# Gated mix of an S4 convolution and a sigmoid GLU: the inverse stage of two pieces in one visit, the first unit fed part by part, results stored in halves, and a new order of work

## The chip, the cores and the metric

The kernel runs on one core of a Trainium2 chip. The metric is the device time of one execution in microseconds (us); less is better. The engines of the core are TensorE (PE, with PEld for its weight loads), VectorE (DVE), ScalarE (ACT), GpSimd (POOL) and SyncE (SP). In this kernel SP issues nearly all transfers (DMAs), and POOL issues the accumulating ones. L12 is line 12 of the kernel; the changed kernel has other line numbers, and where a row of it is shown, the line of before is named beside it.

## The reference

All is in float32. The sequence has 2048 rows of 512 channels, the GLU has 1792 hidden columns, and the state of the convolution has 128 modes for each channel.

```python
g = sigmoid((x * gate_w).sum(-1, keepdims=True))
# a: S4 convolution
dt = exp(log_dt)[:, None];  logdA = dt * A;  dB = dt * Bc
K  = einsum("dn,dnl,dn->dl", Cc, exp(logdA[:, :, None] * l), dB).real      # l = 0 .. 2047
y  = irfft(rfft(u padded) * rfft(K padded))[:, :2048] + u * Dskip
# b: GLU
h = sigmoid(x @ w_gate) * (x @ w_up);   b = h @ w_down
out = g * a + (1 - g) * b
```

The sum over the modes for the table K, the transform, the product with K's transform and the transform back are a; the three large products are b.

## The kernel before

**The GLU.** The 2048 rows are worked in two halves of two blocks (sb 0 and 1) of 512 rows, the hidden columns in 14 groups f of 128. A unit is one (half, sb, f): gate and up (tile `gups`, L947), a sigmoid and a product (L964 on ACT, L966 on DVE), and h (L970, L971). Each float32 operand of the large products is held as a high and a low part, and three matmuls (high by high, high by low, low by high) make one product; so a unit has 2 x 4 x 3 = 24 matmuls of 128x512 on `gups`, and 56 units have 1344. The down product (`dps`, L999) has 672 more of that shape. A loaded 128x512 block lies in a staging tile `st` (DMA L864); ACT writes the high part (L868), DVE the low part (L869).

**The sums.** Down's result for a group of f is scaled by 1 - g and added to a row tile `acc` (L1015 and L1022 on ACT with an accumulating DMA of POOL, L1024; for the last group of the second half L1035 on DVE). Rows of the first half are kept in a buffer in memory and fetched again as `al`.

**The convolution.** The table of K is made by DVE and ACT (`steps`, `pp`, `T`, `B`, `ex`), PE (`kps` L527, `wps` L555) and stored to `a_k`; u's first transform (`ups` L606) is stored to `a_u`. Then come two passes, one for each 256 channels, of 8 pieces p each. A piece loads the constants `wwu` (SP, L653) and `wwv` (L671) and its data `au` (two DMAs, L658) and `ak` (two DMAs, L667); PE makes `s2u` (L688), which is copied to `uf` (L297); PE makes `s2k` (L713), and DVE multiplies the two (L724, L725, L730, L731); PE makes the inverse `ips` (L751) into four banks of PSUM, which are copied to `ev` (L297) and stored to `b_s` (L766). At the end of a pass come the finals: `b_in` is loaded (L789), PE makes `fps` (L801) of it, and DVE adds g times that to the rows: to `al` (load L809, sum L810, store `out<-al` L814) for the first half, and to `acc` (L817) for the second half. What comes last on a row tile of the second half stores it whole (`out<-acc`, 128x512, L829).

These small matmuls use a part of the array each (64x32, 32x64 and so on), while `gups` and `dps` use all of it. A run of `gups` or `dps` is called a full run here, and a run of the others a small run. PSUM's eight banks are three for `gups`, one for `dps` (later it also gets those of `gups`), and four (named XB in the code) for all small tiles.

**The order.** Every part of the work is a generator that yields one step at a time with an engine, a cost, a function and its dependencies. A planner (`Plan.run`) takes the next step of a kind and engine as a table of letters (`ORDER`) says; so the table sets the order of each engine's instructions and of the DMAs in SP's queue. Costs and dependencies only choose which waiting step of a kind is taken and which slot of a buffer it gets. An engine works its queue strictly in this order: if an instruction waits, those behind it wait too, and so do SP's DMAs. The waits themselves go by data and slots.

Of the kernel before, what the change touches and what calls it, by code (L numbers as in the profile page):

```python
# [26 lines left out]
AF = mybir.ActivationFunctionType  # L27
# [24 lines left out]
TURNS = ("ustep PE", "ustep ACT", "ustep -", "inv PE", "inv ACT", "inv SP", "inv -", "x SP", "w SP", "split ACT", "split DVE",  # L52
         "rows PE", "rows ACT", "rows DVE", "rows SP", "rows -", "dn SP", "urest ACT", "urest DVE", "urest SP", "bases ACT",
         "bases DVE", "bases -", "tables PE", "tables DVE", "tables -", "first PE", "first ACT", "first DVE", "first SP", "first -",
         "mags ACT", "mags DVE", "hidden PE", "post ACT", "post DVE", "down PE", "add ACT", "add DVE", "add SP", "add POOL",
         "passes SP", "step PE", "step DVE", "step -", "finals SP", "last PE", "last DVE", "last SP", "last -", "const SP",
         "steps DVE", "steps SP", "preludes ACT", "preludes DVE", "preludes SP", "pw SP", "splitw ACT", "splitw DVE", "splitw SP",
         "splitd ACT", "splitd DVE", "splitd SP")
ORDER = (
    "HJ0zKI56HJzKHJKh4HJhKIQI56hhhhh8zHI56IhhhIHij0JKHQH56ihhJK56h3h3JK569JijKj2hh7ij1y2VVyWPhQh8ijOhhU8VhNijhi9UMPj9UkUyLUVR"  # L60
    "kklhPURhiYOg7YIh5ffikNMIYY6YYjkPLRPONghgklhYhRjgMTg5ikkPLPhVik7VWTIY56hhUYVTjlhUIihkhUkkYYYUYjiYRYONRMPLP3OYN5MPUZIyLTSX"
    "jlkkRhjVTU6iIYgk6PYOhYh55hYbceQNYTYSfj7fgihglRjkaig8kbMkYb!jIhgVlVhiP6YLWUhhhbTPONbVYYkYY9Y5UYYYZi6kMPUTRRUhjILUVPXkj3hh"
    "T!UYi7lOTjY5iYYgYIfjYYfYhRbRNkgTIg7gcYkhQij8hMPe9LPO6kYQ5hgijTRR5hViT6ablhYNbh8hVWbUMPYTbLVhiPkONhhYUYYMTjh!RUYP9kZjXUUT"
    "ViL6UYgRkijjYhhbcQ89kf2Peh!dT6fggOYg1lkkkkgRRiajNlkkYkkib2YYVhbIhhiYMPIVh5YlbkkW5UT6YVbYLUTPONMUPUYRTYL6UYYYYhojRRVoUk7k"
    "IlIRZXbjiYg5fhckjekh7PkYYYkflaoYkYYkohk5YYikYggghbgbhbblVVWU7kI5jhhYiVihUYYYYkYkUUkUoTjIjZXTlk6hiVU6iYh5gffYYjdkIhYYQO8k"
    "Yh6YNMPLYhihhPONRYRjhgiggbgVjVWUk9TMhioYj!yPLhhQ8VYIPcl9eiTRRaYONYk6hh!jQ89!YUQYMih8jTkUbYZXUiPUjjb9iVjb7UYk!YkgLYbYTY5P"
    "lIShYbcfkShkY6hYkefgggkg35oIaYViOoh5lkkVWUk5N6MPT7khIbbVh!7YYhUbiTlkkYYkYYYZLUU6jX6SUVbj5bkl6U!cehYg3RhijkkY2fkhYY12ofTg"
    "YkYlgagkkokkihilkokgdYIboVYYhVbkbWk56UbhVhYYlk!ohUiYUjkToYYjHkYUQUYj8oVkiT9lUZhXQ8jYhgJYYhYQ87bcikYYf9YeaYKHfjog9bbhTkhb"
    "kghibJgl7hHgoJkYVVWkHkYhiUYVlkYojYkKYhYIhYjZUUdpppppUKhUVhpJijiXKQjUCbkYglnYIABBsqppppkYphhceHrYkrHfrfggikrabGYgYhbbjbhY"
    "DEYIYpEhEgVijCHVYWEFJKHABBisqlrhnFprpJhkkUpkVphoprJrihjGUjUDhUnYYYhCKEloEkkJUkYoEYKEFABBYsVUZliqrX!kk3bYgpkYiKp!YrcFfYhe"  # L70
    "rhphjaplfkirYkgYoYpbpjhg3bGbjbDpEEEgYEhCgVVWiiABBQsqrFUVhklrYppprUhFYppQhIhirGYYkUDCEEEYEpFjYhdjjUABYBsqUkrkiiYrnjhpoplV"
    "rFUZhXYbghjY2YhfhckYrYekfYiakYgg12YbgpYlGpgbYhnVbbkVkk!lYDCEpEEYphkkiWUVYAnjEFBBsYFqUiYklpphphjUkpYoZrrprkkrUlXkbckUVGIj"
# [66 lines left out]
class Plan:  # L139
# [62 lines left out]
    def run(self):  # L202
        order, owed = iter(ORDER), []
        turns = dict(zip(LETTERS, TURNS))
        while True:
# [27 lines left out]
            _, n, _, deps = st[2]  # L233
            m = n[eng] if isinstance(n, dict) else n
# [876 lines left out]
```

## Time and profile before

| what | before |
|---|---|
| median of three runs | 625.27 us (624.94 to 626.48) |
| the profiled execution | 625.42 us |
| its span (first to last instruction) | 623.7 us |
| PE busy, share of the span | 608.8 us, 98% |
| DVE busy | 506.4 us, 81% |
| ACT busy | 429.4 us, 69% |
| DMA bytes | 140.34 MB, 225 GB/s on the mean |

The span is the time from the first instruction to the last, and 1.7 us of the profiled execution lie around it. The execution is 0.15 us above the median. A busy time of PE counts modelled ends of pipelined matmuls, so the timeline's starts, not its durations, give the time that a group of matmuls takes. In the timeline a matmul of the small tiles is counted twice as often as in the order lists below (an inverse of 16 matmuls is an `x32`); `gups` and `dps` count alike in both.

### The profile page before, as it was taken

The numbers are of one execution on the slowest core, as the hardware profiler recorded it, in microseconds if no ns is written. First come the engines' busy times: TensorE is split into PE (matmuls) and PEld (weight loads), VectorE is DVE, ScalarE is ACT, GpSimd is POOL, SyncE is SP. The second block draws the span as 40 slices with busy tenths as digits, with TensorE's granted clock in tenths as the row PEclk, the third lists the DMA queues.
The fourth block names the chain that finished last, engine by engine and source line by source line (L and its number), as shares of the span: only waits on it lengthen the run. The fifth ranks groups of instructions, "written<-read, shape, count | busy, mean of one in ns | idle before, by whom it ended". The sixth has DMA issues, their size and how long they took to land.

```text
span 623.7 us, 16354 instructions
## 1 busy us (share of the span) xinstructions
PE 608.8 (98%) x6816; PEld 461.0 (74%) x6816; DVE 506.4 (81%) x902; ACT 429.4 (69%) x726; POOL 35.1 (6%) x44
## 2 busy tenths in 40 slices
PE   5999999999999999999999999999999999998997
PEld 3877777787777778877776777777787776775775
DVE  5879899999999999999999999998986163663145
ACT  5597988989989798988878687767684233342210
POOL 0000000010100111010110000000201000110000
PEclk9999999999999999999999999999999999999999
DMA  7844866588759498698999678777856999999875
GB/s 226 287 161 122 288 204 200 182 234 272 219 158 292 134 295 255 197 294 239 209 261 281 202 214 211 244 236 227 236 151 180 229 224 264 247 231 235 256 224 178
DMA packets 97161, 140.34 MB, mean 225 GB/s; under 512 B 40000, under 2 KB 65472, under 8 KB 92480
## 3 DMA queue, kind: packets, MB, share of 16 engines
q1 hardware_dynamic: 91328, 128.81, 67.9%
q0 software_dynamic: 5760, 10.49, 10.1%
q8 instruction: 54, 0.88, 0.6%
q14 instruction: 19, 0.16, 0.1%
HBM read 75.31 MB, written 53.48 MB: 207 GB/s over the span
## 4 chain that ended last, share of the span: by engine, by line
PE 87%; DVE 6%; DMA 3%; ACT 1%; SPq 1%; issue 1%; DVEq 0%; ACTq 0%
PE gups L947 45%; PE dps L999 23%; PE kps L527 5%; PE wps L555 3%; PE ups L606 3%; PE fps L801 2%; PE s2u L688 2%; PE s2k L713 2%; PE ips L751 2%; DMA b_s<-ev 1%; DMA ak<-a_k 1%; DMA st<-wgu 1%; SPq L658 1%; DVE uf L725 0%; DVE tt L724 0%
## 5 line engine op out<-in xcount | busy, mean ns | idle before, releaser
L947 PE MATMUL gups<-x,gu 128*128 128x512 f32 x1344 | 332.6, 396 | 7.5 <-ACT gu L868 6.5
L947 PEld LDWEIGHTS gups<-x,gu 128*128 128x128 f32 x1344 | 250.7, 189 | 76.8 <-issue 12.7
L999 PE MATMUL dps<-dnw,h 128*128 128x512 f32 x672 | 175.9, 397 | 0.0
L999 PEld LDWEIGHTS dps<-dnw,h 128*128 128x128 f32 x672 | 123.1, 188 | 35.2 <-issue 9.0
L1024 POOL DMA_DIRECT2D acc<-part x40 | 34.9, 871 | 549.6 <-ACT part L1022 365.9
L970 ACT ACTIVATE h<-sg 128x512 fp32r<-128x512 f32 x56 | 34.9, 627 | 28.5 <-DVE sg L966 28.5
L477 ACT ACTIVATE B<-B 128x32 f32<-128x32 f32 (+2 forms) x96 | 53.3, 669 | 0.4
L971 DVE TENSOR_TENSOR h<-sg,h 128x512 fp32r<-128x512 f32 x56 | 38.3, 685 | 17.7 <-ACT h L970 17.7
L724 DVE TENSOR_TENSOR tt<-s2k,uf 128x512 f32<-128x512 f32 x32 | 21.9, 686 | 35.2 <-PE s2k L713 34.7
L461 DVE TENSOR_TENSOR T<-T,t 128x64 f32<-128x64 f32 (+4 forms) x80 | 46.5, 581 | 1.2
L459 DVE TENSOR_TENSOR t<-T,bz 128x64 f32<-128x64 f32 (+4 forms) x80 | 46.1, 576 | 1.2
L460 DVE TENSOR_TENSOR T<-T,bz 128x64 f32<-128x64 f32 (+4 forms) x80 | 46.2, 577 | 0.0
L966 DVE TENSOR_TENSOR sg<-gups,sg 128x512 f32<-128x512 f32 x56 | 38.0, 683 | 9.5 <-PE gups L947 5.8
L1022 ACT ACTIVATE part<-dps,omg 128x512 f32<-128x512 f32 x40 | 27.4, 684 | 23.6 <-PE dps L999 23.4
L297 ACT ACTIVATE ev<-ips 128x256 f32<-128x256 f32 x64 | 20.0, 387 | 33.4 <-PE ips L751 20.9
L964 ACT ACTIVATE sg<-gups 128x512 f32<-128x512 f32 x56 | 33.6, 601 | 13.2 <-PE gups L947 12.9
L565 ACT ACTIVATE kev<-wps 128x256 f32<-128x256 f32 x64 | 34.8, 643 | 5.6 <-PE wps L555 5.6
L527 PEld LDWEIGHTS kps<-B,T 128*32 128x32 f32 x2048 | 29.4, 110 | 7.4 <-issue 5.0
L527 PE MATMUL kps<-B,T 128*32 128x64 f32 x2048 | 31.9, 220 | 0.3 <-DVE T L461 0.2
L297 ACT ACTIVATE uf<-s2u 128x512 f32<-128x512 f32 x32 | 17.4, 595 | 18.6 <-PE s2u L688 18.5
L430 ACT ACTIVATE af<-ex 128x1216 int32<-128x1216 f32 x16 | 19.6, 1228 | 15.0 <-DVE ex L421 13.4
L431 DVE TENSOR_TENSOR ex<-ex,af 128x1216 f32<-128x1216 f32 x16 | 22.7, 1418 | 0.7 <-ACT af L430 0.5
(85 smaller groups left out, 684.0 us busy)
## 6 DMA issues: line engine op xcount, KB each, us to landing
wsp<-gu SPq DMA_DIRECT2D x14, 1024.0 KB, 6.9
gu<-wsp SPq DMA_DIRECT2D x14, 1024.0 KB, 7.7
acc<-part POOLq DMA_DIRECT2D x40, 256.0 KB, 6.0
a_u<-evu SPq DMA_DIRECT2D x32, 256.0 KB, 4.4
a_k<-kev SPq DMA_DIRECT2D x8, 1024.0 KB, 5.0
au<-a_u SPq DMA_DIRECT2D x32, 256.0 KB, 6.0
ak<-a_k SPq DMA_DIRECT2D x32, 256.0 KB, 6.7
b_s<-ev SPq DMA_DIRECT2D x32, 256.0 KB, 4.1
```

The source lines that it names most:

```text
L297: copy = lambda eng, out_, in_: A.activation(out_, in_, AF.Copy) if eng == "ACT" else V.tensor_copy(out_, in_)
L459: yield "DVE", dve(n), lambda: V.tensor_tensor(t2, src, sb, op=OP.mult), [t, slot.t]
L460: t = yield "DVE", dve(n), lambda: V.tensor_tensor(dst, src, br, op=OP.mult), [t]
L461: t = yield "DVE", dve(n), lambda: V.tensor_tensor(dst, dst, t2[:, :, ::-1], op=OP.add), [t]
L477: A.activation(B[:, :, 0, 1 << k::2 << k], B[:, :, 0, 1:64 >> k:2], AF.Exp, scale=float(1 << k))
L527: mm(p[32 * jj:32 * jj + 32, s], T[:, ch, c], B[:, ch, c], start=(c == 0), stop=(c == 1), tile_position=(0, 32 * jj), skip_group_check=True)
L947: mm(p, gu[:, a, k, dc], x[:, b, dc], start=(dc + n == 0), stop=(dc == NC - 1 and n == 2))
L966: t = yield "DVE", dve(512), lambda: V.tensor_tensor(sg, pu, sg, op=OP.mult), [t, tu]
L970: t = yield "ACT", act(512), lambda: A.activation(h[:, 0], sg, AF.Copy), [t, hs.t]
L971: t = yield "DVE", dve(512), lambda: V.tensor_tensor(h[:, 1], sg, h[:, 0].bitcast(F32), op=OP.subtract), [t]
L999: mm(p, h[:, a, 128 * s:128 * s + 128], dn[:, b], start=(f == f0 and n == 0), stop=(f == f0 + gn - 1 and n == 2))
L1024: ts = yield "POOL", kb(430), lambda: nc.gpsimd.dma_start(accs[t], part, accum_op=OP.add), [te, begun[t]]
```

## The change

1. **Inverse.** In the second pass the inverse of pieces p - 1 and p is one visit of PE, when both are ready: the four banks hold `[128, 2, 256]` each, one half for each piece. There are four visits of 32 matmuls in that pass in place of eight of 16; the first pass keeps its eight. The copies to `ev` are a strand of their own (`evict`), may be done by ACT or DVE, and the banks come free with the copies of the second piece. Each of the 64 copies of L297 on `ev` was on ACT; now 44 are on ACT and 20 on DVE. A slot of `wwv` and of `uf` is held until the visit of its pair.
2. **First unit.** In unit (0, 0, 0), gate and up go on together over x's four parts: part 0 for gate, part 0 for up, part 1 for gate, and so on, in two open banks. Before, all four parts went into gate and then all four into up, and the weight's second block was loaded only after x.
3. **Results in halves.** `finished` stores a row tile's columns 0 to 255 and 256 to 511 each when its own two sums are done: 16 stores of 128x256 in place of 8 of 128x512. In the order laid out, both stores of a tile stand one behind the other in SP's queue.
4. **Engines and costs.** Copies of `kst` and `kev` and the sums of L1022 may go to ACT or DVE by the planner's choice; in the order laid out all of them stay where they were, with 40 accumulating DMAs of POOL as before. Some costs in the planner (`ldt`, `pw`, `gwb`, and a transfer's slack in the first 8 us) are others.
5. **The order** is another from the first letter to the last.

No matmul is added or taken away. Over all of PE's rows, a full run follows a small run 79 times before and 73 times after.

At the start, SP's first loads were x, `ldt` (for the tables), the weight's first block, x twice, `pw`, x; now they are `ldt`, weight, x, weight, x, w_down, x, weight, x, and `pw` comes 19th. On DVE thirteen small operations on `steps` now stand ahead of x's first low part, where five did.

On PE, in the first pass (`s2u`, `s2k` and `ips` are a piece's three visits, `kps` and `wps` belong to the table of K). Before:

```order
L751 MATMUL ips<-uf,wwv 64x256 x16
L947 MATMUL gups<-x,gu 128x512 x6
L688 MATMUL s2u<-au,wwu 32x256 x16
L713 MATMUL s2k<-ak,wwu 32x256 x16
L999 MATMUL dps<-dnw,h 128x512 x6
L947 MATMUL gups<-x,gu 128x512 x12
L527 MATMUL kps<-B,T 32x64 x64
```

After, for a piece at that place (L692 is L688 of before, L717 is L713):

```order
L763 MATMUL ips<-uf,wwv 64x256 x16
L1032 MATMUL dps<-dnw,h 128x512 x3
L692 MATMUL s2u<-au,wwu 32x256 x16
L955 MATMUL gups<-x,gu 128x512 x6
L1032 MATMUL dps<-dnw,h 128x512 x6
L955 MATMUL gups<-x,gu 128x512 x6
L717 MATMUL s2k<-ak,wwu 32x256 x16
```

Here 18 full matmuls now stand between `s2u` and `s2k`, where none did; the next piece but one has nine there.

On PE, at the last pieces of the second pass. Before:

```order
L999 MATMUL dps<-dnw,h 128x512 x6
L947 MATMUL gups<-x,gu 128x512 x12
L751 MATMUL ips<-uf,wwv 64x256 x16
L999 MATMUL dps<-dnw,h 128x512 x9
L751 MATMUL ips<-uf,wwv 64x256 x16
L999 MATMUL dps<-dnw,h 128x512 x3
L947 MATMUL gups<-x,gu 128x512 x6
L688 MATMUL s2u<-au,wwu 32x256 x16
L713 MATMUL s2k<-ak,wwu 32x256 x16
```

After, from the third of the four visits to the fourth:

```order
L763 MATMUL ips<-uf,wwv 64x256 x32
L1032 MATMUL dps<-dnw,h 128x512 x12
L692 MATMUL s2u<-au,wwu 32x256 x16
L717 MATMUL s2k<-ak,wwu 32x256 x16
L955 MATMUL gups<-x,gu 128x512 x6
L1032 MATMUL dps<-dnw,h 128x512 x12
L692 MATMUL s2u<-au,wwu 32x256 x16
L717 MATMUL s2k<-ak,wwu 32x256 x16
L955 MATMUL gups<-x,gu 128x512 x6
L1032 MATMUL dps<-dnw,h 128x512 x9
L955 MATMUL gups<-x,gu 128x512 x6
L763 MATMUL ips<-uf,wwv 64x256 x32
```

Two inverses have become one, and the two pieces of a pair follow one upon the other between the visits. In SP's queue the `wwv` of a pair's first piece, whose slot comes free with the visit, now stands ahead of `wwu`, `au` and `ak` of its second piece.

At the end, on SP (the number behind a name tells one buffer from another). Before, the last rows:

```order
L829 DMA out<-acc_4718 128x512
L829 DMA out<-acc_4812 128x512
L814 DMA out<-al_7582 128x256
L829 DMA out<-acc_4946 128x512
L814 DMA out<-al_7610 128x256
L829 DMA out<-acc_5206 128x512
```

After (L849 is L829 of before, L834 is L814):

```order
L849 DMA out<-acc_4554 128x256 x2
L849 DMA out<-acc_4657 128x256 x2
L849 DMA out<-acc_4786 128x256 x2
L849 DMA out<-acc_4933 128x256
L834 DMA out<-al_7542 128x256
L849 DMA out<-acc_4933 128x256
L849 DMA out<-acc_5063 128x256 x2
L834 DMA out<-al_7592 128x256
L849 DMA out<-acc_5329 128x256 x2
```

And on DVE, after (L837 is L817 of before; the last six sums are on columns 256 to 511; before, each L817 stood ahead of the tile's L1035, and L1035 was last):

```order
L1087 SCALAR_TENSOR_TENSOR acc_5329<-dps_7577,omg_88,acc_5329 128x512
L837 SCALAR_TENSOR_TENSOR acc_4554<-fps_7538,g_87,acc_4554 128x256
L837 SCALAR_TENSOR_TENSOR acc_4657<-fps_7538,g_87,acc_4657 128x256
L837 SCALAR_TENSOR_TENSOR acc_4786<-fps_7612,g_87,acc_4786 128x256
L837 SCALAR_TENSOR_TENSOR acc_4933<-fps_7612,g_87,acc_4933 128x256
L837 SCALAR_TENSOR_TENSOR acc_5063<-fps_7620,g_87,acc_5063 128x256
L837 SCALAR_TENSOR_TENSOR acc_5329<-fps_7620,g_87,acc_5329 128x256
```

PE's last runs were `fps` x8 and `dps` x33; they are now `dps` x45 and then `fps` x12, that is three banks of `fps`, on which those six sums wait. The second store of each of these six tiles waits on its sum.

The diff, cut to its core (the table of letters is left out but for its first line):

```diff
-    "HJ0zKI56HJzKHJKh4HJhKIQI56hhhhh8zHI56IhhhIHij0JKHQH56ihhJK56h3h3JK569JijKj2hh7ij1y2VVyWPhQh8ijOhhU8VhNijhi9UMPj9UkUyLUVR"
+    "211K7JLM8jK7JL8jMjSJKL1MJK!7K8LjjMj780#jjk7lk2jj8JK78jLMjJklJ5j5jLM43S!j6Jlj0R4XXjkLLYMMSjkjjWX!QlWkjPjOR5llWklW9WNT#mkm"
...
-        t = yield "SP", kb(2), lambda: S.dma_start(x, ldt), []
+        t = yield "SP", kb(150), lambda: S.dma_start(x, ldt), []
...
+        waits[j, p] = wvs, wwv, ufs, uf, t
+        two = j == NW - 1
+        if two and p % 2 == 0:
+            return
+        parts = [p - 1, p] if two else [p]
+        t = max(waits[j, q][4] for q in parts)
         yield near(t)
         banks = yield XB, 4
-        pi = [b.tile("ips", [P, w]) for b in banks]
+        pi = [b.tile("ips", [P, 2, w]) for b in banks]
...
-        t = yield "PE", ("32x64", 3.6e-3 * w, 65.8), mms, [t] + [b.t for b in banks]
-        wvs.free(t)
-        ufs.free(t)
+        t = yield "PE", ("32x64", len(parts) * 3.6e-3 * w, len(parts) * 65.8), mms, [t] + [b.t for b in banks]
+        for i, q in enumerate(parts):
+            waits[j, q][0].free(t)
+            waits[j, q][2].free(t)
+            plan.spawn(evict(j, q, [x[:, i] for x in pi], banks, q < p, t), "inv")
+
+    def evict(j, p, pi, banks, hold, t):
...
-            banks[i].free(t1)
+            if hold:
+                banks[i].t = max(banks[i].t, t1)
+            else:
+                banks[i].free(t1)
...
-    def finished(t, te):
-
-        summed[t].set(te)
-        oleft[t] -= 1
-        if oleft[t] == 0:
-            yield "SP", kb(256), lambda: S.dma_start(out[t], accs[t]), [summed[t].t]
+    def finished(t, j, te):
+
+        oleft[t][j] -= 1
+        if oleft[t][j] == 0:
+            cols = slice(OFF[j], OFF[j + 1])
+            yield "SP", kb(WIDTHS[j] / 2), lambda: S.dma_start(out[t, :, cols], accs[t][:, cols]), [te]
...
+                    if (half, sb, f) == (0, 0, 0):
+                        banks = []
+                        for k in range(2):
+                            bank, = yield GU, 1
+                            banks.append((bank.tile("gups"), bank))
+                        ends = [None, None]
+                        for dc in range(NC):
+                            for k in range(2):
+                                yield wr[0][k]
+                                gu, gs = wr[1]
+                                yield xr[0][dc]
+                                x, xsl = xr[1]
+                                p, bank = banks[k]
+                                ends[k] = t = yield "PE", ("f", 3 * 0.227, 6.02), partial(mms, p, gu, x, k, dc, 1), [
+                                    bank.t, wr[0][k].t, xr[0][dc].t]
...
-            yield from finished(t, te)
+            for j in range(NW):
+                yield from finished(t, j, te)
```

More of the change, by code (lines that the diff above doesn't have):

```diff
@@ L51 @@
 LETTERS = "ABCDEFGHIJKLMNOPQRSTUVWXYZabcdefghijklmnopqrstuvwxyz0123456789!#$%&()*+,-./:;<=>?@"
[L52 to L58, printed above, removed]
@@ L625, in urest @@
             E["rows"].set(max(end))
-    fin = {}
+    fin, waits = {}, {}
     bdone = [Ev() for _ in range(NW)]
@@ L934, in hidden, with mms @@
                     pp = []
[L935 to L950 removed]
+                    def mms(p, gu, x, k, dc0, m):
+                        for dc in range(dc0, dc0 + m):
+                            for n, (a, b) in enumerate(((0, 0), (0, 1), (1, 0))):
+                                mm(p, gu[:, a, k, dc], x[:, b, dc], start=(dc + n == 0), stop=(dc == NC - 1 and n == 2))
```

143 lines of the change are left out of this document (84 added, 59 removed).

## The prediction

> **What bounds the kernel now.** I read the page's head and chain first, then the groups by line.
>
> ```profile
> span 623.7 us, 16354 instructions
> PE 608.8 (98%) x6816; PEld 461.0 (74%) x6816; DVE 506.4 (81%) x902; ACT 429.4 (69%) x726; POOL 35.1 (6%) x44
> PE 87%; DVE 6%; DMA 3%; ACT 1%; SPq 1%; issue 1%; DVEq 0%; ACTq 0%
> ...
> L947 PE MATMUL gups<-x,gu 128*128 128x512 f32 x1344 | 332.6, 396 | 7.5 <-ACT gu L868 6.5 <-DVE x L869 0.8 <-ACT sg L964 0.3
> ```
>
> PE is the bound: 98% of the span, 87% of the chain. Its named idle time is small: 6.5 us ahead of the first matmul, 0.8 soon after, 0.3 in one more place by this row, and 0.7 and 2.2 in two places of the passes that come below; behind its last matmul the span has a tail (below). DVE at 81% and ACT at 69% have room on the mean. So the time after is PE's work, plus its price for changing between full and small runs, plus start, waits and tail. The work stays. I sum against the profiled execution, 625.42 us, which stands 0.15 above the median of 625.27. About 0.3% (1.9 us) is what a measurement of this kernel can tell from no change.
>
> **Term 1, the changes of mode.** The matmul by itself is read from a long run of the chain, the change from the starts at the end of the second pass.
>
> ```profile
> 483.90 12.24 PE gups L947 x54
> ...
> 558.96 1.12 PE L751 MATMUL ips<-uf,wwv 32*64 32x256 f32 x32
> 560.01 2.34 PE L999 MATMUL dps<-dnw,h 128*128 128x512 f32 x9
> 562.28 1.12 PE L751 MATMUL ips<-uf,wwv 32*64 32x256 f32 x32
> ...
> 564.13 1.54 PE L947 MATMUL gups<-x,gu 128*128 128x512 f32 x6
> 567.86 1.37 PE L688 MATMUL s2u<-au,wwu 64*32 64x256 f32 x32 [2.19 <-ACT ev L297]
> 568.99 1.46 PE L713 MATMUL s2k<-ak,wwu 64*32 64x256 f32 x32
> 570.37 1.67 PE L947 MATMUL gups<-x,gu 128*128 128x512 f32 x6
> ```
>
> One full matmul takes 12.24 / 54 = 0.227 us. The nine `dps` after an inverse take 562.28 - 560.01 = 2.27, against 9 x 0.227 = 2.04: each full run behind a small one costs 0.23 more. There are 79 such returns, and 73 after: 6 x 0.23 = -1.4. Four inverse visits also merge. No row shows an inverse of double length; the nearest is the finals, double and single:
>
> ```profile
> 600.54 3.67 PE L801 MATMUL fps<-b_in,wf 128*64 128x256 f32 x32
> 604.14 5.73 PE L999 MATMUL dps<-dnw,h 128*128 128x512 f32 x24
> 609.80 1.95 PE L801 MATMUL fps<-b_in,wf 128*64 128x256 f32 x16
> 611.68 7.77 PE L999 MATMUL dps<-dnw,h 128*128 128x512 f32 x33
> ```
>
> Two single runs take 2 x 1.88 = 3.76, the double one 3.60, so a merge saves 0.16, and four 0.6. The term is -2.0, with -1.4 as the upper end (a merge saves nothing by itself) and -2.3 as the lower (it saves as much as a return). The doubled hold of the banks is priced among the rivals.
>
> **Term 2, the start.**
>
> ```profile
> 6.47 2.08 PE L947 MATMUL gups<-x,gu 128*128 128x512 f32 x4 [6.47 <-ACT gu L868]
> 9.37 21.80 PE L947 MATMUL gups<-x,gu 128*128 128x512 f32 x86 [0.82 <-DVE x L869]
> ...
> 9.40:12.40 3.00, 3.00 (x7) 2.42 (x8) 1.00 0.97 367
> 12.40:15.40 3.00, 3.00 (x12) 2.36 (x12) 1.00 0.68 220
> 18.00:21.00 3.00, 3.00 (x15) 2.48 (x14) 1.00 0.43 109
> ...
> 4.30 0.17 DVE L326 TENSOR_SCALAR steps<-steps 16x32 f32<-16x32 f32 x1 [3.43 <-DMA steps<-ldt]
> 4.50 0.17 DVE L327 TENSOR_SCALAR steps<-steps 16x32 int32<-16x32 f32 x1
> 5.23 0.67 DVE L869 TENSOR_TENSOR x<-st,x 128x512 fp32r<-128x512 f32 x1
> ```
>
> The three windows count `gups` (second number in brackets: weight loads; then clock, DMA share, GB/s). Matmuls start 0.43 us apart at first (7 in 3.0 us) and 0.2 later (15); 12 in the middle window puts the change near 13.4, and the granted clock reads 1.00 throughout. The first matmul still needs a high part of the weight and of x, so it stays near 6.5. With gate and up taking turns, each part of x feeds six matmuls instead of three, so PE should run on where it stopped at 8.55. Before, by 13.4, 4 + 4.0 / 0.43 = 13 had started; without a stop from 6.5 on it is 6.9 / 0.43 = 16. Three more, at 0.227 each of later time, are 0.7; I take -0.5. Against it: thirteen operations on `steps`, 0.2 apart, now stand ahead of x's first low part. From a landing 0.45 earlier they end near 3.85 + 2.6 = 6.5, and that low part comes 1.3 later than at 5.23. The second matmul needs it at 6.9 and gets it at about 7.2. If each later part is late too, I put the loss at most at those 1.3, less the 0.3 that one place earlier in the queue gives: +1.0 is the upper end. The lower end is worked out with the second rival.
>
> **Term 3, the tail.**
>
> ```profile
> 603.40 1.74 DVE L817 SCALAR_TENSOR_TENSOR acc<-fps,g,acc 128x256 f32<-128x256 f32 x4 [1.82 <-PE fps L801]
> 610.94 0.48 DVE L817 SCALAR_TENSOR_TENSOR acc<-fps,g,acc 128x256 f32<-128x256 f32 x1 [0.95 <-PE fps L801]
> 619.49 0.75 DVE L1035 SCALAR_TENSOR_TENSOR acc<-dps,omg,acc 128x512 f32<-128x512 f32 x1 [0.90 <-PE dps L999]
> ...
> 610.39 0.42 SPq L809 DMA_DIRECT2D al<-acc  x1
> 610.87 0.45 SPq L814 DMA_DIRECT2D out<-al  x1
> 611.42 0.38 SPq L809 DMA_DIRECT2D al<-acc  x1
> 620.27 0.33 SPq L829 DMA_DIRECT2D out<-acc  x1
> ...
> out<-al SPq DMA_DIRECT2D x16, 128.0 KB, 2.2
> out<-acc SPq DMA_DIRECT2D x8, 256.0 KB, 2.1
> ```
>
> Now PE ends at 611.68 + 7.77 = 619.45, one sum of 0.75 follows, one store is issued at 620.27, and the span ends 3.4 later, at 623.7: a tail of 4.2. After the change three banks of `fps` end PE: call their start F. Twenty-four records at 3.60 / 32 are 2.7, so PE ends at F + 2.8. The first sum on them starts 1.14 after such a run's start (610.94 - 609.80) and takes 0.48: F + 1.6. Only then can SP issue the second store of `acc_4554`, and twelve DMAs stand behind it. Back to back, SP's issues start 0.48 apart (610.39, 610.87), so the last goes at F + 1.6 + 12 x 0.48 = F + 7.4, and the span ends at F + 10.8: a tail of 8.0, +3.8. I take +3.5, since an issue itself can be a little shorter (0.33 at 620.27). Smaller stores don't win it back: 128 KB land in 2.2 us and 256 KB in 2.1. The lower end: if issues did not queue, the last of six sums at 1.74 / 4 each would end at F + 1.1 + 2.6 = F + 3.7, and the span at F + 7.2, a tail of 4.4: +0.2. The upper end, at 0.55 (610.87 to 611.42) an issue, is +4.6.
>
> The Trainium skill, "DMA: Bandwidth & Descriptors", section "Rules for kernel authors", says to coalesce many small transfers; by it alone halves lose. The two medians agree that half the bytes take as long, but the whole of the loss I forecast lies in SP's issues, and without these the sum would be 621.7.
>
> **Term 4, the waits in the passes.**
>
> ```profile
> 337.63 0.59 PE L713 MATMUL s2k<-ak,wwu 64*32 64x256 f32 x2
> 338.88 1.09 PE L713 MATMUL s2k<-ak,wwu 64*32 64x256 f32 x30 [0.66 <-DMA ak<-a_k]
> 339.90 1.66 PE L999 MATMUL dps<-dnw,h 128*128 128x512 f32 x6
> ...
> 330.60 8.15 DMA ak<-a_k
> ...
> 558.64 3.89 SPq L667 DMA_DIRECT2D ak<-a_k  x2
> ...
> ak<-a_k SPq DMA_DIRECT2D x32, 256.0 KB, 6.7
> ...
> L297 ACT ACTIVATE ev<-ips 128x256 f32<-128x256 f32 x64 | 20.0, 387 | 33.4 <-PE ips L751 20.9 <-issue 6.5 <-DMA b_s<-ev 6.0
> ```
>
> Two places go. At 337.6 `s2k` takes 2.27 to the next run, against 339.90 - 338.88 = 1.02 for nearly all of it: 1.2 lost, since `ak` took 8.15 to land. After, 18 full matmuls (4.1 us) stand between `s2u` and `s2k` there, which covers it. At 564.13 six `gups` should take 1.4, but `s2u` begins at 567.86: 2.2 idle, and with its own late end 2.3, because banks waited for copies that waited for an old store of `ev` (the 6.0 us of `b_s` in ACT's row); `s2k` then lost 0.35 to its `ak`. The two inverses that stood 3.3 us apart are one, so that pile-up goes. Together -3.9.
>
> What is late next: `ak` of a pair's second piece. Its loads stand on SP behind a `wwv` that waits for the visit, so they start when the visit ends: `wwv`, `wwu` and two of `au` at 0.48 each, then two `ak` at 3.89 / 2 each. The second is issued 1.9 + 1.9 = 3.9 after the visit and lands 6.7 later, at 10.6. PE reaches that `s2k`, by the third visit's rows, after 30 full matmuls (6.8), two returns (0.5) and three small visits at about 1.0: at 10.3. So it is a tie, and with a landing of 8.15 instead of 6.7 it waits 1.7. There are three such places; I take 0.6 each, +1.8, with ends of 0 and 5.1. A new order also has small waits that no row can name; before had the 0.3 from the table's last entry of `gups`, and I add +1.0, ends 0 and 2. Term 4 is -1.1.
>
> **Sum.** -2.0 - 0.5 + 3.5 - 1.1 = -0.1: 625.3 us, no change that can be measured.
>
> Costed at nothing: ACT's copies that go to DVE (20), covered by DVE's idle 19%; without that cover they cost, at ACT's 0.39, 20 x 0.39 = 8 us of DVE, of which PE sees what delays a bank. The planner's costs move nothing but the order.
>
> **The rivals.**
>
> *Faster: the tail stays small.* SP's issues don't queue as I count, for instance since the sums come one by one and each store goes as its sum ends. It decides from the last `fps` run on: below 0.25 an issue the queue is no longer the limit. The time is 625.3 - 3.3 = 622.0. For it: stores to `out` of 0.33 us at 620.27. Against: starts 0.48 apart in the rows above. Chance 0.17.
>
> *Faster: matmuls speed up earlier.* Slow spacing ended about 4.0 us after the run from 9.37 began. If the speed needs 4.0 us without a stop, a start without a stop at 6.5 is fast from 10.5: the 2.9 us until 13.4 then hold 2.9 / 0.2 = 14 in place of 7, and seven matmuls at 0.227 are 1.6, so term 2 is about -2.0 and the time 623.8 (with small gains elsewhere, faster). The Trainium skill, "TensorE: Matmul & The Clock Gate", Part 1, says that the array runs at half rate until a window of about 3.4 us saw it busy, and that the window runs freely; by it the warm-up could come within one such window. The 4.0 us here agree in size, but no row shows the gate itself. Chance 0.12, most of it for a time under 623.4.
>
> *Slower: the second pass is starved.* All three `ak` land in 8.15 or later, or the copies of two pieces (eight at 0.39 on ACT alone, 3.1 us) hold the banks beyond the 2.9 us of 12 full matmuls behind the third visit. The point from which it decides is a second `ak` issued later than 3.6 us after the visit. Then 3 x 1.7 = 5.1 stands in place of 1.8: 628.6. For it: the 3.89 that two issues of `ak` took at 558.64, which is a queue held up. Against: DVE shares the copies, and SP is idle while it waits, so transfers then start on free queues. Chance 0.30. If the start also loses its 1.0, 629.
>
> **How the numbers follow.** Forecast 625.3: chance 0.38. Tail small 0.17, early speed 0.12, starved 0.30; the rest, 0.03, is spread. Faster than by 0.3%: 0.17 + 0.10 + part of the rest = 0.29. Slower: 0.30 and a little of the forecast's own upper side = 0.34. Same: 0.37. The likeliest case's own range is 623.6 to 627.0. With both kinds of rivals inside, the range is 621.2 to 629.0.
>
> **What would show it.** Step 1: 73 returns with the same 0.23, and inverse runs of 64 records near 1.95 us. Step 2: no stop at 8.5 and 16 matmuls by 13.4; a stop longer than 0.8 would refute it. Step 3: SP's last twelve issues back to back after the first of six sums, and a tail near 7.7; a tail under 5 refutes it. Step 4: `s2k` of pieces four, six and eight of the second pass with `ak` as releaser, 0 to 1.7 each, and no wait for `ev` copies. I am wrong at large if PE shows new idle time above 5 us in a place not named here, such as the tables of K behind the earlier order.

## The result, and the profile after

| what | before | after |
|---|---|---|
| median | 625.45 us (624.94 to 626.48, 4 runs) | 636.24 us (635.77 to 637.25, 4 runs) |
| ratio to before | | 1.0173 (1.0154 to 1.0191) |
| the profiled execution, its span | 625.42 us, 623.7 us | 636.01 us, 634.2 us |

The changed kernel is 1.7% slower; the forecast was no change. The head of its page, and the row of the granted clock in 40 slices of the span:

```profile
span 634.2 us, 16370 instructions
PE 613.9 (97%) x6816; PEld 464.4 (73%) x6816; DVE 517.1 (82%) x927; ACT 423.8 (67%) x704; POOL 35.1 (6%) x44
...
PEclk9999999999999999977999999999999999999998
```

The matmuls are the same 6816, but PE is busy for 5.1 us longer, and the clock's row has two slices at 7. Both point to one place. It shows in windows, whose columns are the length, then busy time and count of PE, PEld, DVE, ACT and POOL, the granted clock, the DMA share and GB/s. Before, from 275.2 to 293.0:

```profile
275.20:293.00 17.80, 17.80 (x355) 12.97 (x361) 17.39 (x35) 14.53 (x29) 0.89 (x1) 1.00 0.99 287
```

After, the same stretch:

```profile
275.20:293.00 17.80, 12.40 (x90) 6.67 (x83) 8.50 (x18) 8.56 (x16) 0.89 (x1) 0.62 0.90 233
```

PE starts 90 matmuls there, DVE and ACT stand idle for half of it, and the mean clock is 0.62. PE's timeline after, at that place, which is the first piece of the first pass:

```profile
275.22 1.65 PE L955 MATMUL gups<-x,gu 128*128 128x512 f32 x6
280.20 1.08 PE L692 MATMUL s2u<-au,wwu 64*32 64x256 f32 x8 [3.33 <-DMA st<-xt]
282.06 1.93 PE L692 MATMUL s2u<-au,wwu 64*32 64x256 f32 x24 [0.78 <-DMA au<-a_u]
...
286.31 1.96 PE L717 MATMUL s2k<-ak,wwu 64*32 64x256 f32 x30 [0.71 <-DMA ak<-a_k]
288.19 2.93 PE L1032 MATMUL dps<-dnw,h 128*128 128x512 f32 x6
290.92 2.27 PE L955 MATMUL gups<-x,gu 128*128 128x512 f32 x6
293.03 0.85 PE L1032 MATMUL dps<-dnw,h 128*128 128x512 f32 x3
```

From 275.22 to 293.03 are 17.8 us. Full speed would need 18 full matmuls at 0.227 (4.1), two small visits (1.9) and two returns (0.23 each), 6.4 in all; so 11.4 are lost. PE waits for the piece's data. These come late, as SP's queue shows, after:

```profile
262.26 0.32 SPq L573 DMA_DIRECT2D a_k<-kev  x1
274.97 0.33 SPq L657 DMA_DIRECT2D wwu<-c_wwu  x1
```

and before (L653 is L657 of after):

```profile
263.82 0.33 SPq L569 DMA_DIRECT2D a_k<-kev  x1
264.37 0.33 SPq L653 DMA_DIRECT2D wwu<-c_wwu  x1
```

The first `wwu` of the passes is issued 0.55 after the store ahead of it before, and 12.7 after it now. (The releaser `st<-xt` that the first row of `s2u` names is the transfer that happened to land last; `s2u` reads `wwu` and `au`.) What SP waited for, after, from the waits of its queue between 250 and 295, and DVE's timeline there:

```profile
SPq L657 <- DMA acc<-part: 8.9, 1, 8.9
...
SPq L657 <- DVE x L887: 3.3, 1, 3.3
...
274.26 0.68 DVE L887 TENSOR_TENSOR x<-st,x 128x512 fp32r<-128x512 f32 x1
```

A load of `wwu` has no data in common with an accumulation of `acc` or with the low part of x. It shares a place with their buffers. `passes` closes the buffer pool `early` (the tables' `steps`, `u`, `evu`, `ju`, and three extra staging slots `se`, which serve as `st` for weights and x and as `part` for the accumulations) and opens the pool `fin` in its room. The tile framework lets the first tile of `fin` wait for the last readers of all that lay in `early`. The waits fit this: SP waits until 271.6 for an accumulation of a `part` (issued at 268.38 on POOL, landed 3.2 later), and then for a part of x for the second half, which DVE split at 274.26 to 274.95. SP issued `wwu` at 274.97. Before, the last split ahead of the load ended at 261.8, before SP came to the load at all, so the same wait cost nothing. DVE's row of before:

```profile
261.13 0.69 DVE L869 TENSOR_TENSOR dnw<-st,dnw 128x512 fp32r<-128x512 f32 x1
```

That these slots are the cause is so far an argument from the waits; the experiment with a pool of their own tests it.

The planner does not see this wait: it gives the slots of `fin` the time zero.

The start, after (the first stretch on PE, and two windows with `gups` alone: PE, PEld, clock, DMA share, GB/s):

```profile
5.99 28.08 PE L955 MATMUL gups<-x,gu 128*128 128x512 f32 x108 [5.99 <-ACT x L886]
34.00 1.13 PE L610 MATMUL ups<-u,wu 64*128 64x512 f32 x4
...
9.40:12.40 3.00, 3.00 (x8) 2.42 (x8) 1.00 0.59 200
12.40:15.40 3.00, 3.00 (x14) 2.43 (x14) 1.00 0.76 215
```

The second pass, after: an inverse of two pieces, and one of three `s2k` that take longer than the 1.0 of an undisturbed one (568.63 - 566.51 = 2.1; the others, at 552.69 and 573.82, take 1.7 and 1.3); the row of 567.61 names DVE, but that piece's second `ak`, issued at 558.33, landed at 567.47, just ahead of it:

```profile
519.95 1.98 PE L763 MATMUL ips<-uf,wwv 32*64 32x256 f32 x64
521.86 1.65 PE L955 MATMUL gups<-x,gu 128*128 128x512 f32 x6
...
566.51 0.59 PE L717 MATMUL s2k<-ak,wwu 64*32 64x256 f32 x2
567.61 1.09 PE L717 MATMUL s2k<-ak,wwu 64*32 64x256 f32 x30 [0.50 <-DVE uf L298]
568.63 1.65 PE L955 MATMUL gups<-x,gu 128*128 128x512 f32 x6
```

The end, after, on PE, DVE and SP:

```profile
623.43 2.81 PE L821 MATMUL fps<-b_in,wf 128*64 128x256 f32 x24
...
624.56 2.60 DVE L837 SCALAR_TENSOR_TENSOR acc<-fps,g,acc 128x256 f32<-128x256 f32 x6 [0.27 <-PE fps L821]
...
625.07 2.78 SPq L849 DMA_DIRECT2D out<-acc  x6
...
630.62 0.95 SPq L849 DMA_DIRECT2D out<-acc  x2
```

PE ends at 623.43 + 2.7 = 626.1; SP's thirteen last issues stand back to back from 625.07 to 631.6, and the span ends at 634.2: a tail of 8.1.

The account of the 10.6 us between the two spans:

| place | forecast | measured | read from |
|---|---|---|---|
| changes of mode (term 1) | -2.0 | -2.1 | what the others leave |
| start (term 2) | -0.5 | -1.1 | the first 108 `gups` are over at 34.00, before at 35.08 |
| tail (term 3) | +3.5 | +3.8 | 8.1 against 4.3 by the same reading |
| waits in the passes (term 4), but for the next row | -1.1 | -1.4 | -3.9, three late `s2k` for +0.7, +1.1 and +0.3, and +0.4 in small waits |
| the first piece of the first pass | (in term 4's +1.0) | +11.4 | the rows above |

### The profile page after: what moved, and what is told of

Read it like the earlier page. It is cut to its first block, busy times and chain, and to the rows that moved or that the text cites. A ratio compares the mean times of both kernels' runs of the same rounds, so it can differ in the third digit from the quotient of the medians.

```text
span 634.2 us, 16370 instructions
## 1 busy us (share of the span) xinstructions
PE 613.9 (97%) x6816; PEld 464.4 (73%) x6816; DVE 517.1 (82%) x927; ACT 423.8 (67%) x704; POOL 35.1 (6%) x44
## 4 chain that ended last, share of the span: by engine, by line
PE 85%; DVE 8%; ACT 2%; DMA 2%; issue 1%; SPq 1%; DVEq 0%; ACTq 0%
PE gups L955 44%; PE dps L1032 23%; PE kps L528 4%; PE ups L610 3%; PE s2k L717 2%; PE wps L557 2%; PE s2u L692 2%; PE fps L821 2%; PE ips L763 2%; DMA ak<-a_k 1%; DVE T L462 1%; DVE T L461 1%; DVE t L460 1%; DMA st<-xt 1%; DVE uf L729 1%
## 5 line engine op out<-in xcount | busy, mean ns | idle before, releaser
L955 PEld LDWEIGHTS gups<-x,gu 128*128 128x128 f32 x1344 | 251.5, 190 | 72.4 <-issue 11.6
L1032 PEld LDWEIGHTS dps<-dnw,h 128*128 128x128 f32 x672 | 124.5, 189 | 37.2 <-issue 9.8
L298 ACT ACTIVATE uf<-s2u 128x512 f32<-128x512 f32 x28 | 15.7, 594 | 36.0 <-PE s2u L692 36.0
L298 ACT ACTIVATE ev<-ips 128x256 f32<-128x256 f32 x44 | 14.6, 387 | 27.3 <-PE ips L763 25.1
L431 ACT ACTIVATE af<-ex 128x1216 int32<-128x1216 f32 x16 | 19.6, 1224 | 11.8 <-DVE ex L422 10.5
L435 ACT ACTIVATE af<-ex 128x1216 f32<-128x1216 f32 x16 | 19.6, 1223 | 6.0 <-DVE ex L432 5.7
```

Source lines behind the costliest of these rows:

```text
L298: copy = lambda eng, out_, in_: A.activation(out_, in_, AF.Copy) if eng == "ACT" else V.tensor_copy(out_, in_)
L955: mm(p, gu[:, a, k, dc], x[:, b, dc], start=(dc + n == 0), stop=(dc == NC - 1 and n == 2))
L1032: mm(p, h[:, a, 128 * s:128 * s + 128], dn[:, b], start=(f == f0 and n == 0), stop=(f == f0 + gn - 1 and n == 2))
```

## The experiments

The theory at the start of them: the stop costs 11.4 by itself; it comes from the room that the first load takes over; the other terms are as forecast. The rivals: PE merely lacks other work in front of the late data (then other work put there covers it); the data would be late anyway, for lack of traffic room; the tail, not the stop, is the larger part.

### The staging slots given back early

The three slots leave the staging list one step before the last, so that no late tile gets one of them, and one load of x moves behind a load of `ak`:

```diff
         rleft[0] -= 1
+        if rleft[0] == 1:
+            del ST[-len(more):]
         if rleft[0] == 0:
```

> The changed kernel, but the three extra staging slots are given back when the last but one block of u is copied, so that the first load of the pass (wwu) has no late reader to wait for; one load of x goes behind that piece's ak. All other queues keep their order. Theory (the wait of that load on the slots' last readers costs 11.4 us): wwu is issued near 263 instead of 274.97, PE does not stop near 277, its clock stays at 1.00, and the time is about 625. Rival (the stretch is bound by DVE, 98% busy there, and the stop only moves): PE stops later in the same stretch and the time stays above 632.

Measured: 630.04 us (627.68 to 633.47, 8 runs), ratio 1.0072 (1.0036 to 1.0109). `wwu` was issued at 262.51, as the theory says it should be, and 6 of the 11 us came back. It is no clean test, though: with three staging slots fewer SP stood behind loads that had no slot, `wwu` and the first `au` took 12.6 and 14.2 us to land, and a new stop came further on. PE's timeline of this kernel:

```profile
299.34 1.09 PE L719 MATMUL s2k<-ak,wwu 64*32 64x256 f32 x30 [2.34 <-DMA ak<-a_k]
```

### The first piece put later

`s2u` and `s2k` of the first piece go behind some 27 and 36 more full matmuls, by moving two letters (`A` and `s`) in the table; the loads stay as late as they are.

```diff
-    "...rraianlJrDArBBrusrhthmamt...rarmL"
-    "ijkilJqirE...
+    "...rraianlJrDrBBrurhthmamt...rAarmLi"
+    "jskilJqirE...
```

> The changed kernel with wwu as late as it is, but s2u and s2k of the first piece of the first pass stand 27 and 36 full matmuls later on PE. Theory (PE only lacks other work there): the stop at 277 is covered, the clock stays up, about 625. Rival (DVE or the loads bind the stretch as a whole): the stop comes at the next pieces, above 632.

Measured: 638.11 us in one run: nothing won. The matmuls that were moved ahead cover most of the first wait, but the piece's `ips` then stands right behind its `s2k`, and waits for the products between them:

```profile
295.40 0.65 PE L763 MATMUL ips<-uf,wwv 32*64 32x256 f32 x6 [2.58 <-issue]
296.99 2.81 PE L763 MATMUL ips<-uf,wwv 32*64 32x256 f32 x26 [0.94 <-DVE uf L729]
```

So the stop is not a missing piece of work in front of one visit. All that follows from the piece is late, and this one layout did not hide the delay; others were not tried.

### Matmuls in the gap

To part the wait itself from what it does to PE's clock, matmuls whose result nobody uses stand ahead of the first `s2u`: 80 in a first try, 40 in a second (twice that in the profile's records).

```diff
+        if ready is seen[0]:
+            for i in range(40):
+                x = i % 2
+                mm(pu[0][64 * x:64 * x + 64, 0], wf, wk..., tile_position=(0, 64 * x))
```

> The changed kernel with 80 more matmuls of 128x64 by 256 columns, whose results are overwritten, ahead of the first s2u of the first pass, so that PE is busy (some 9 us) while it waits. The outputs do not change. If the slow matmuls after the stop (0.4 us apart, granted clock 0.50) come from PE having been idle, those after the wait run at full speed, and of the 11.4 us about 2.8 go: near 633.4. If they come from late operands or from something else, the time stays within 0.5 of 636.2.

Measured: 646.05 us in one run. The 80 matmuls took 17.4 us, far more than the wait; they delayed `s2u` themselves, and the run says nothing on the question.

> As the first run with matmuls for the waiting PE, but 40 of them: the first had 80, which by the trace take 17.4 us, twice the wait. Forty take 8.7 us and end near 285.4, when au has landed and ak is about to. If the slow matmuls after the stop come from PE having been idle, s2u and s2k take about 1 us each and the two full runs behind them lose nothing: 2.8 of the 11.4 us go, near 633.4. If not, those runs stay slow and the time stays at 636 or above.

Measured: 646.77 us in one run. Two windows and the timeline of PE in the kernel with 40:

```profile
280.00:284.00 4.00, 4.00 (x42) 2.63 (x39) 0.00 (x0) 0.00 (x0) 0.00 (x0) 1.00 1.11 205
...
289.17 1.66 PE L1040 MATMUL dps<-dnw,h 128*128 128x512 f32 x6
...
292.05 0.84 PE L1040 MATMUL dps<-dnw,h 128*128 128x512 f32 x3
...
358.19 0.42 PE L528 MATMUL kps<-B,T 128*32 128x64 f32 x12 [3.47 <-issue]
```

With PE at work through the gap (the 40 start at 277.00 and give way to `s2u` at 285.79) the clock stays at 1.00, and the twelve full matmuls behind `s2k` take 292.05 - 289.17 = 2.9 us; in the changed kernel they take 293.03 - 288.19 = 4.8 at a clock of 0.50. So 1.9 of the 11.4 is the price of having stood still, paid after the data were there, and the last 30 records of `s2k` add 0.9 (286.31 to 288.19 is 1.9, 288.15 to 289.17 here 1.0). The whole time cannot be used: stops of 3.5 and 3.1 us came at two `kps` that had none (the last row is one), and what makes these stops was not settled.

### Half of the last stores on ACT's queue

```diff
-            ... lambda: S.dma_start(out[t, :, cols], accs[t][:, cols]), [te]
+            ... lambda: (A if j else S).dma_start(out[t, :, cols], accs[t][:, cols]), [te]
```

> The changed kernel with the stores of columns 256 to 511 issued from ACT's queue, which is empty at the end, and the others from SP as before. Theory (twelve issues of SP stand behind the first late sum and make the tail 8.0): the last store is issued as the last sum ends, the tail falls to about 4.4, the time to about 632.6. Rival (landing of many half stores, or the sums, make the tail): it stays near 636.2.

Measured: 633.25 us (632.67 to 639.76, 4 runs, three of them within 1.1), 3.0 below the changed kernel. By its interval, 1.0101 to 1.0226, the ratio is not apart from the changed kernel's, because of the one run at 639.76; so the reading rests on the trace. The stores of columns 256 to 511 now stand alone on ACT's queue, each some 0.5 behind the last. PE and ACT at the end:

```profile
622.51 2.81 PE L821 MATMUL fps<-b_in,wf 128*64 128x256 f32 x24
...
624.16 3.26 ACTq L849 DMA_DIRECT2D out<-acc  x6
```

PE ends at 625.2, 0.9 earlier than in the execution of the changed kernel, and the span ends at 630.7: a tail of 5.5 instead of 8.1. So 2.6 of the 3.8 that the tail had grown by are SP's issues; the theory had 4.4 for what is left of the tail. Two kernels that follow bear it out in their traces: with the slots in a pool of their own the tail is 8.6 while all these stores are on SP, and 5.0 and 5.1 in two executions with half of them on ACT's queue. The Trainium skill, "DMA: Bandwidth & Descriptors", section "Rules for kernel authors", says that spreading DMAs over several issuing engines gives no bandwidth and saves only the issue time of the sequencer. The trace agrees on the issue time, 2.6 us here; bandwidth was not measured.

### The staging slots in a pool of their own

The test of the cause. Every engine's order stays as it is in the changed kernel. The three slots get a pool above `early`, which is closed with it, and of the tiles of `fin` only `ev` and `al`, which are used later, lie in the room that these slots held:

```diff
+    stage = pool("stage")
+    stg = stage.__enter__()
...
-    more = slots(erl, "se", 3, [P, 512])
+    more = slots(stg, "se", 3, [P, 512])
...
+        stage.__exit__(None, None, None)
         early.__exit__(None, None, None)
         fp = ctx.enter_context(pool("fin"))
+        fp2 = ctx.enter_context(pool("fin2"))
...
-            fin[n] = slots(fp, n, k, s)
+            fin[n] = slots(fp2 if n in ("ev", "al") else fp, n, k, s)
```

> The changed kernel with the three extra staging slots in a pool of their own, above the early one, so that wwu's place is no longer freed by their last readers. All engines keep exactly the order of the changed kernel, and all slots their sizes. Theory (the wait on the staging slots' last readers, 11.4 us, is the whole of what the forecast missed): wwu is issued near 263, no stop at 277, clock 1.00, time about 636.2 - 11.4 = 624.8. Rival (the loads of that stretch saturate the queues when they start earlier, as in the first try, where wwu and au took 12.6 and 14 us to land): 628 to 630.

Measured: 625.55 us (623.08 to 627.96, 10 runs), ratio 0.9986 (0.9959 to 1.0013): 10.7 below the changed kernel. SP and PE at the place, and a window as above:

```profile
262.78 2.13 SPq L661 DMA_DIRECT2D wwu<-c_wwu  x1
...
275.37 1.65 PE L959 MATMUL gups<-x,gu 128*128 128x512 f32 x6
276.95 1.10 PE L696 MATMUL s2u<-au,wwu 64*32 64x256 f32 x32
...
281.70 0.84 PE L1036 MATMUL dps<-dnw,h 128*128 128x512 f32 x3
...
276.00:280.00 4.00, 4.00 (x74) 2.67 (x73) 3.93 (x11) 3.50 (x11) 0.89 (x1) 1.00 0.85 292
```

`wwu` is issued right behind the store of `a_k`, `s2u` follows the `gups` without a stop, and the clock holds 1.00. The stretch that took 17.8 us takes 281.70 - 275.37 = 6.3. No instruction was moved: where the slots lie was the whole of the 11.4.

### The final sums ahead of the last down products

On top of the last kernel, the table's end is laid out so that the last `fps` come before the last 27 `dps` (some sixty letters of the table's last two lines).

> The same with the tail mended as well: the last three banks of fps stand ahead of the last 27 full matmuls, and each sum of fps ahead of the tile's last sum of dps, so only two stores stand behind the last sum. Theory: the tail falls from 8.1 to about 4.7, time 624.8 - 3.4 = 621.4, and it beats the kernel before by some 4. Rival (the tail is set by landings, not by SP's queue): no better than the run above.

Measured: 625.96 us (623.16 to 628.12, 10 runs), ratio 0.9997 (0.9974 to 1.0020); the tail is 7.6, no better than it was. Two accumulations of POOL had come to stand behind sums on `fps`, and the last two sums of DVE wait for these, 2.1 and 1.5 us, with eleven stores behind them on SP; POOL's row and the last sum:

```profile
609.66 1.76 POOL L1080 DMA_DIRECT2D acc<-part  x2 [52.12 <-DVE acc L841]
...
615.27 0.75 DVE L1091 SCALAR_TENSOR_TENSOR acc<-dps,omg,acc 128x512 f32<-128x512 f32 x1 [1.46 <-DMA acc<-part]
```

The miss comes from the experiment's own edit; it does not speak against term 3. A second layout, in which the two accumulations come ahead:

> Pools apart as in e_pool, and the tail mended again. In b_all two accumulating DMAs of POOL had come to stand behind sums of fps on the same tiles (issued at 609.7 and 610.3), the last sums waited for them, and twelve stores stood in SP's queue behind an out<-al that waited; here the accumulations stand first and that al store last. Theory (the tail is what SP's queue and the last sum make it): tail about 5.1 in place of 8.5, time 625.5 - 3.4 = 622.1. Rival (the landing of many half stores): a tail of 7 or more.

Measured: 623.14 us (621.30 to 625.90, 10 runs), ratio 0.9977 (0.9946 to 1.0008), tail 6.0: fourteen half stores stood in one row on SP from 611.8 to 620.1, so their queue was still the limit. That lies between the theory's 5.1 and the rival's 7.

### The first unit as before

From the kernel with the final sums ahead, gate and up one after the other again:

```diff
-                        for dc in range(NC):
-                            for k in range(2):
+                        for k in range(2):
+                            for dc in range(NC):
```

> The run above with the first unit as before the change: all four parts of x into gate, then into up; the loads keep the changed order. By term 2 the turns of gate and up are worth 0.6 (the stop of 0.8 us comes back): about 622.0. Rival (the changed order of the loads gives all of it): within 0.3 of the run above.

Measured: 627.87 us (625.89 to 629.83, 10 runs), ratio 1.0028 (1.0006 to 1.0050), 1.9 above the kernel it was made from, where 0.6 was expected. PE's start, and the window from 12.4 to 15.4 with `gups` alone:

```profile
8.80 2.38 PE L959 MATMUL gups<-x,gu 128*128 128x512 f32 x4 [0.17 <-ACT x L890]
11.77 18.43 PE L959 MATMUL gups<-x,gu 128*128 128x512 f32 x70 [0.59 <-DVE x L891]
...
12.40:15.40 3.00, 3.00 (x9) 2.24 (x8) 1.00 0.70 203
```

Two stops come back, 0.17 and 0.59, and the window holds 9 matmuls where it holds 15 with the parts shared. By the starts of single matmuls, they are 0.43 apart until 16.6 here, and until 11.6 in the kernel that it was made from; the nineteenth starts at 16.62 against 13.22. So the two profiled executions differ by 3.4 at the start, and the medians by 1.9: a stop costs more than its length, since the fast spacing comes later too. A part of the 3.4 is chance: in the kernels that share the changed start, the fast spacing came 4.4 to 6.6 us after the run began.

### The inverses apart

From the same kernel, the second pass's inverses one piece a visit again (`two = False`), each first one put where its piece is about ready:

> The run of all three mends with an inverse visit for each piece in the second pass too, six to eighteen full matmuls apart. By term 1 four more returns and fixed parts cost 4 x (0.23 + 0.16) = 1.6: about 623.0. Rival (the visit of a pair holds wwv, so that loads start late, and that costs the 2.1 us of waits for ak seen in the changed kernel): those waits go, and the time is 621.0 or less.

Measured: 632.62 us (630.92 to 633.87, 4 runs), ratio 1.0105 (1.0061 to 1.0148). The first inverse of each pair was put too early. A pair on PE, and the double visit of the kernel it was made from:

```profile
507.01 0.65 PE L767 MATMUL ips<-uf,wwv 32*64 32x256 f32 x6
508.73 1.10 PE L767 MATMUL ips<-uf,wwv 32*64 32x256 f32 x26 [1.07 <-DVE uf L733]
509.76 3.03 PE L959 MATMUL gups<-x,gu 128*128 128x512 f32 x12
512.72 1.12 PE L767 MATMUL ips<-uf,wwv 32*64 32x256 f32 x32
513.77 1.66 PE L959 MATMUL gups<-x,gu 128*128 128x512 f32 x6
```

```profile
508.85 1.98 PE L767 MATMUL ips<-uf,wwv 32*64 32x256 f32 x64
510.77 1.65 PE L959 MATMUL gups<-x,gu 128*128 128x512 f32 x6
```

The first visit takes 509.76 - 507.01 = 2.75 instead of 1.05 (512.72 to 513.77); over the four pairs that is 6.8 of waiting. From the `s2k` ahead of the first pair (496.74, and 495.87 with double visits) to the end of the last inverse (578.27, and 568.92) it is 81.5 us against 73.1, 8.5 more. The 1.7 that the waits leave are four times 0.42: two visits of 1.05 and one more return of 0.23, less the 1.92 of a double visit. So a merge is worth 0.42 in this pass, 0.23 of it the return and 0.19 the visit.

### Both repairs together

The slots in their own pool, and half of the last stores on ACT's queue, with the changed kernel's order:

> Pools apart as in e_pool, all orders as in the changed kernel, and the stores of columns 256 to 511 from ACT's queue as in e_act. If the two mends add up: 625.5 - 2.8 = 622.7, with a tail of 5.5 as in e_act.

Measured: 622.75 us (621.69 to 624.94, 10 runs), ratio 0.9976 (0.9949 to 1.0002). The same kernel in a second series:

> The kernel with pools apart and the late half stores on ACT's queue once more, in more rounds, since its interval reached 1.0002. Theory (terms 1 and 2 are worth 3 us, the tail costs 1, the waits are even): 2 us under the kernel before, a ratio of 0.997 with an interval under 1. Rival (the gains are eaten by the stops for ak in the second pass): 1.000.

Measured: 621.58 us (620.04 to 624.44, 12 runs), ratio 0.9949 (0.9925 to 0.9972) to a before of 624.96. Its PE, at the end:

```profile
612.08 2.81 PE L825 MATMUL fps<-b_in,wf 128*64 128x256 f32 x24
```

PE ends at 614.8 and the span at 619.9. The first interval just reaches 1, the second leaves it out. With its two losses taken away the change is a gain: 3.4 us below before in the second series, and 14.7 below the changed kernel's median, which is of another series.

## Why the prediction was wrong, point by point

**Term 1, the changes of mode: right.** -2.0 forecast, -2.1 left over by the others. The double visit takes 521.86 - 519.95 = 1.91 against twice 1.05, so a merge saves 0.19 where 0.16 was read from the finals, and the inverses apart show a return of 0.23 more. Six returns at 0.23 and four merges at 0.19 are 2.1 as well.

**Term 2, the start: right in sign, forecast at half its size.** -1.1 by PE's timeline against -0.5. The stop at 8.5 is gone, as forecast, the first matmul starts at 5.99 instead of near 6.5, and the matmuls start 0.43 apart until 12.6 and 0.23 apart behind that. So 18 had started by 13.4, where the step counted 16 and before had 14: four times 0.227 is 0.9. The two that the step lacked come from the speed, which rose 0.8 earlier than in before: a part of the second rival, though not its 10.5. The loss that was set against the gain did not come: `ldt` landed by 2.28 instead of 3.85, the steps on DVE were out of the way, and x's first low part began at 5.97, right behind its high part. The -1.1 is that of one execution: in eleven more traces with this start the first 108 `gups` are over between 33.5 and 34.6. (The rival of a starved pass has a slip: a start that loses 1.0 instead of winning 0.5 makes 628.6 into 630.1, and not 629.)

**Term 3, the tail: right.** +3.8 against +3.5: SP's thirteen issues in a row, 0.51 apart on the mean where 0.48 was counted. The half on ACT's queue takes 2.6 of the tail away, which leaves the rival of a small tail no room.

**Term 4, the waits: near in the sum of those it named, partly by luck, and wrong where it named none.** Both stops of before are gone. `s2k` is late in three places, for 0.7, 1.1 and 0.3, 2.1 in all against +1.8 forecast, each time until 0.14 after its second `ak` landed; the starved second pass, the slower rival, did not come. But the three places are pieces six, seven and eight of the pass, and the step named four, six and eight. Piece four lost nothing, and the largest loss is at seven, the first piece of a pair, whose `ak` was issued before the visit and took 9.1 us to land. So the mechanism holds for two of the places, and the sum is near by luck. In the kernels with double visits and without the stop in the first pass, the three pieces lose from 0.1 (final sums ahead) to 3.4 in all (its second layout), and 3.1 and 1.5 in two executions of the kernel with both repairs. The cover of 18 matmuls at the first of the two old stops is only just enough, too: in the kernel with the slots in their own pool that `s2k` again loses 0.8, since its `ak` took 9.4 to land.

**The step that failed is the last of term 4: "A new order also has small waits that no row can name", +1.0, ends 0 and 2.** In its place stands one wait of 11.4 us. A row could have named it: the load of `wwu` stands in the queue of before at 264.37, takes over the room of another pool, and so waits for the last reader of everything there. Who that is follows from the order of the changed kernel, since the three staging slots go to whatever asks for one. So a wait goes not only by a tile's data and slot, but also by the room of a closed pool. The prediction read SP's queue for what stands ahead of a load, and not for whose place the load takes. Its closing sentence on idle time "in a place not named here" is what happened, at the start of the first pass. Without this, the kernel is at 0.9986 of before (0.9959 to 1.0013), that is 0.9 us less with 0.8 more to 2.6 less in the interval, and the forecast sum of -0.1 lies in it; the start and the places of the `ak` waits show that this sum is not right in every part.

## What to carry to other kernels

Where an order is laid out anew, look for every load that takes over the room of something else and list that room's last readers in the new order: where a whole pool is replaced, the first tile waits for the last reader of any slot in it, staging slots lent out to others among them, and a planner that starts the new slots at time zero does not see it. Split stores only where their issues have a free queue, since behind the last sum each one costs its issue (0.51 us here). And a stop of the main engine is paid for twice, as idle time and as slow matmuls behind it, so read the granted clock there before the rest of a loss is looked for elsewhere.

## What the runs showed of the hardware that was not expected

**The clock falls sooner than it comes back.** PE's last matmul ahead of the stop ended at about 276.9. A window from 278.5 to 279.0 has a granted clock of 0.83 and the next has 0.50, so it fell near 278.8, after some 2 us without a matmul. By a window from 292 to 293 at 0.76 it came back near 292.5, when PE had worked without a gap since 286.3, for 6.2 us. At 0.50 full matmuls start 0.43 us apart (289.21, 289.64, 290.07), which is the spacing of the start as well, though the clock's row reads 1.00 there. From the last stop to the fast spacing the start took 4.2 us before, 6.6 after, 5.4 with the final sums ahead and 4.8 with the first unit as before. A stop of 2.2 us in the second pass of before left the clock at 1.00, and so did 3.2 us without a matmul (276.85 to 280.08) at this very place in the kernel with half of the stores on ACT's queue, where the clock fell near 281.3.

The Trainium skill, "TensorE: Matmul & The Clock Gate", Part 1, says that the clock rises when a window of about 3.4 us saw the array busy, and that these windows run freely. From this I estimate that the first whole busy window ends 3.4 to 6.8 us after a run begins; all five times above lie in that. Its section "HAM oscillation — how this bites in real kernels" puts the fall at idle gaps of more than about 3.4 us; here it fell after 2 in one execution, and did not fall in gaps of 2.2 and 3.2 in others, so the length of the gap alone does not decide.

**Landing times hang on the crowd.** The first two `au` of 256 KB took 4.4 and 4.7 us to land in the changed kernel, and 14.2 and 14.6 in the kernel with the staging slots given back, where SP had issued eight other transfers in the 8.4 us before them. The DMA share over the first `au` was 0.58 in the one and 1.01 in the other.

**What stays open.** The stops of 3.5 and 3.1 us at `kps` in the kernel with extra matmuls have no releaser in the profile. And single runs of one kernel lie up to 7.5 us apart in the later series (621.82 to 629.36 for before), where the first had 1.5. The traces of the kernels with the changed start show that start ending up to 1.0 us apart; the rest of the spread is not explained.
